# Sums of the first MLP that stay in PSUM, a weight remainder on another engine, and a finer-grained passage into the second MLP

## The chip, the cores and the metric

The kernel runs on one core of one Trainium2 chip. The metric is the time of one execution in microseconds (us) on the device; a version is judged by the median of its runs.

The core's engines each work through an instruction list of their own, in order, and wait for each other through semaphores: TensorE (PE; its weight loads are shown apart as PEld), VectorE (DVE), ScalarE (ACT), GpSimd (POOL) and SyncE (SP, which here only issues transfers). Matmul results go to PSUM, which has eight banks here; everything else lies in SBUF.

## What is computed

Attention with a decay bias, then two MLPs, one after the other, over 1152 tokens:

```python
x = attention(q, k, v, s)              # 2 batches, 8 heads of 64, 576 positions -> [1152, 512]
h = x @ w_in                           # w_in [512, 2048], in float64 at the input
g = np.maximum(0.01 * h, h)
x = g @ w_out                          # w_out [2048, 512]
p = domain_probs / (domain_probs.sum(-1, keepdims=True) + 1e-09)
for e in range(4):                     # second MLP: w1 [4, 512, 1024], w2 [4, 1024, 512]
    h = np.maximum(x @ w1[e], 0.0)
    out += p[:, e:e+1] * (h @ w2[e])
```

## The kernel before, in words

**Numbers.** Every float32 matrix is split in two parts: ACT casts it to the type that the matmul reads (`hi`), and DVE or GpSimd subtracts that from the value (`lo`, the remainder). A product is then three matmuls: hi by hi, lo by hi, hi by lo.

**Tokens.** They are cut in two groups, c = 0 (512 tokens) and c = 1 (640 tokens). The first MLP runs for group 0 by plain matmuls of 512 columns, beginning while attention still runs, and after it for group 1. That second pass and the second MLP's up products for both groups, and its down products for group 0, use a scheme in which a 2 by 2 block product takes seven products instead of eight (`block_products`): four PSUM banks, `ps_u0` to `ps_u3` or `ps_d0` to `ps_d3`, receive four products, then three more are added onto banks 0, 2 and 3. Before the fifth may be added, ACT copies bank 0 to SBUF (`tmp`), and DVE makes sums from that copy. The seven forms of the tokens are tiles `t` (of group 0 or 1), made by `paired_steps` from `x` or `y` by subtractions on DVE, casts on ACT and remainders on DVE; each of the seven has two halves, k = 0 and 1. The seven forms of the weights are tiles `w` with remainders made on GpSimd; the weights of the second MLP's down products get eight forms (`eight`), in two halves of four with additions in the raw weights (`raw`) between them.

**Blocks.** An MLP goes in blocks of four rows of 128 of the hidden dimension: four blocks for the first MLP, f = 0, 4, 8 and 12. A block has two up pieces and two down pieces of weights of 512 KB each. `down1` makes the four down results of a block, in the order d = 0, 2, 1, 3, twelve matmuls each for group 0, and DVE adds each to the sum `y` in SBUF (for block 0 ACT copies it). In the program's order for group 0, between the down products of block 8 and those of block 12 stand the up products of block 12's second pair.

**Order.** Until the end of group 0's pass (`fixed = True`) each engine's order is the program's. From there on a scheduler with a model of the engines decides the order on each engine, unless `keep_in_program_order` is asked for. PSUM banks come from three, and after attention from eight (class `Eight`, which deals them out from two pools in turn). SBUF is given out by pools that are opened and closed as a stack; a pool that is opened where others were closed waits for the last use of what lay there. The raw weights of the second MLP have two buffers (`rawp2`).

**Weights of the first MLP.** `supply` converts them from float64 to float32 and writes them to DRAM (`w_f`), and `late_splits` makes hi and lo of those that are read back late, lo on DVE. The last converted piece is the second down piece of block 12.

**Into the second MLP.** The scheduled part ends with `paired_steps` of group 1 on `y`, whose forms `t` of k = 0 and k = 1 are made in equal steps. Then `second` starts: up products for (pair 0, group 0), (pair 1, group 0), (pair 0, group 1), (pair 1, group 1), then the down products. `next_w` calls `fetch`, which keeps two pieces of weights ahead (`look = 2`).

All these calls are issued through one wrapper class, so that the trace names one line, L43, for nearly all: the rows below are told apart by their tiles.

Of the kernel before, what the change touches and what calls it, by code (L numbers as in the profile page):

```python
# [19 lines left out]
def attention_moe_moe2(ctx: ExitStack, tc: tile.TileContext, q, k, v, s, w_in, w_out, probs, w1, w2, out):  # L20
# [7 lines left out]

    fixed = True

    class InOrder:

# [4 lines left out]
        def __getattr__(self, name):  # L39
            call = getattr(self.engine, name)  # L40

            def issue(*args, **kw):
                ins = call(*args, **kw)  # L43
                return tc.keep_in_program_order(ins) if fixed else ins

            return issue

# [31 lines left out]
    const = ctx.enter_context(tc.tile_pool(name="const", bufs=1))  # L79
    first = ctx.enter_context(ExitStack())  # L80
    rawp = first.enter_context(tc.tile_pool(name="rawp", bufs=RAW))
    ypool = first.enter_context(tc.tile_pool(name="ypool", bufs=1))
    dram = ctx.enter_context(tc.tile_pool(name="dram", bufs=1, space=bass.MemoryType.DRAM))

    def f32(ap):
# [42 lines left out]
    def late_splits():  # L128

        nonlocal reading  # L130
        while len(ready) < CONVERTED:
            n = len(ready)
            if n < min(retired + WB + 2, stored):
                reading, raw = True, kept.pop(n, None)
                if raw is None:
                    raw = load_w(*stream[n][:3])
                    for _ in range(5):
                        yield
                while n >= retired + WB:
                    yield  # L140

                w = wpool.tile([P, 2, 1024], F32R, tag="w", name="w")
                for part in (slice(0, 512), slice(512, 1024)):
                    nc.scalar.copy(w[:, 0, part], raw[:, part])
                    nc.vector.tensor_tensor(w[:, 1, part], raw[:, part], f32(w[:, 0, part]), ALU.subtract)
                ready.append(w.rearrange("p l (a b) -> p l a b", a=stream[n][1][0]))
                reading = False
            else:
                yield
# [113 lines left out]
        return w  # L263

    def eight(raw):

        w = wpool.tile([P, 2, 8, 256], F32R, tag="w", name="w")
        b11, b12, b21, b22 = (raw[:, i * 256 : (i + 1) * 256] for i in range(4))

        def split(i):  # L270
            hi, lo = (w[:, l, i : i + 4].rearrange("p s c -> p (s c)") for l in range(2))
            nc.scalar.copy(hi, raw)
            nc.gpsimd.tensor_tensor(lo, raw, f32(hi), ALU.subtract)

        split(0)
        nc.gpsimd.tensor_tensor(b22, b22, b12, ALU.subtract)
        nc.gpsimd.tensor_tensor(b12, b12, b11, ALU.subtract)
        nc.gpsimd.tensor_tensor(b11, b22, b11, ALU.add)
        nc.gpsimd.tensor_tensor(b21, b21, b11, ALU.subtract)
        split(4)  # L280
        return w

    def first_sevens():

# [85 lines left out]
    def in_steps(ps, pairs):  # L370

        for i, ((wh, wl), (xh, xl)) in enumerate(pairs):
            for j, (a, b) in enumerate(((wh, xh), (wl, xh), (wh, xl))):
                nc.tensor.matmul(ps, a, b, start=(i == j == 0), stop=(i == len(pairs) - 1 and j == 2))
# [6 lines left out]
    x_t, y_t, oacc, touched = [], {}, {}, {}  # L381

    def halves(c):
        return ((0, sizes[0]),) if c == 0 else ((0, half[1]), (half[1], sizes[1]))
# [32 lines left out]
    def down1(f, c, h, w):  # L417

        if f == 0:
            y_t[c] = ypool.tile([P, KD, sizes[c]], F32, tag=f"y{c}", name=f"y{c}")  # L420
        for d in (0, 2, 1, 3):
            for lo, hi in halves(c):
                ps = ps_mm.tile([P, 512], F32, tag="mm", name="ps_d")[:, : hi - lo]
                sl, cols = slice(d * P, (d + 1) * P), slice(lo, hi)
                at_h = [at(x, cols) for x in h] if c == 0 else [at(x, j, cols) for x in h for j in range(2)]
                yield from in_steps(ps, [(at(w[i // 2], i % 2, sl), x) for i, x in enumerate(at_h)])
# [9 lines left out]
    def paired_steps(s, of, pool):  # L436

        n = half[s]
        t = t7[s] = pool.tile([P, 2, 7, 2, n], F32R, tag=f"t7_{s}", name=f"t7_{s}")
        for k in range(2):  # L440
            b11, b12 = of[:, k, :n], of[:, k, n:]
            b21, b22 = of[:, 2 + k, :n], of[:, 2 + k, n:]
            sums = scratch.tile([P, 4 * 320], F32, tag="scratch", name="sums")[:, : 4 * n].rearrange("p (s t) -> p s t", s=4)
            def subtract(*args):
                tc.keep_in_program_order(nc.vector.tensor_tensor(*args, ALU.subtract))

            subtract(sums[:, 1], b12, b11)
            subtract(sums[:, 2], b22, sums[:, 1])
            yield
            subtract(sums[:, 3], b22, b12)  # L450
            subtract(sums[:, 0], b21, sums[:, 2])
            yield
            for i, j, x in ((0, 2, of[:, k::2, :n]), (2, 3, of[:, 2 + k : 3 + k, n:]), (3, 7, sums)):
                hi, lo = (t[:, l, i:j, k] for l in range(2))
                nc.scalar.copy(hi, x)
                subtract(lo, x, f32(hi))
                yield

    def paired_up(w, s, leaky):

        n = half[s]
# [3 lines left out]
        bank = block_products("ps_u", n, lambda a, b: [(at(w, a, k), at(x, b, k)) for k in range(2)])  # L465
        if in_sevens:
# [12 lines left out]
        return ht  # L479
# [26 lines left out]

    def block_products(name, n, operands):

        tmp = scratch.tile([P, 2 * 320], F32, tag="tmp", name="tmp")[:, : 2 * n].rearrange("p (i t) -> p i t", i=2)
# [9 lines left out]
        product(0, 0, 0)  # L519
        nc.scalar.copy(u2, bank[0])  # L520
        product(1, 4, 5)
# [53 lines left out]

    def second(blocks):

        w, h = {}, {}

        def up_part(i, pair, s):  # L580
            if (i, pair) not in w:
                (w[i, pair],) = next_w(1)
            h.setdefault(i, ({}, {}))[pair][s] = paired_up(w[i, pair], s, False)

        for pair, s in ((0, 0), (1, 0), (0, 1), (1, 1)):
# [410 lines left out]
    hpool = None  # L996
    look = 2
    t7pool = scratch = None
    last_mlp = False
    x_t.extend((None, ypool.tile([P, KD, sizes[1]], F32, tag="y1", name="x1")))  # L1000
# [76 lines left out]
    with ExitStack() as phase:  # L1077
# [3 lines left out]
        tokens, rest = paired_steps(0, y_t[0], t7early), None  # L1081
        last = 2 * len(phases[1]) + 32 * (len(phases[1]) - 1) + 16
        for i, _ in enumerate(mlps(phases[1])):
            if i >= 12 and i % 6 == 0:
                next(tokens, None)
            if i >= last:
                rest = rest or paired_steps(1, y_t[1], t7pool)
                if i % 4 == 1 and i < last + 16:
                    next(rest)
        for _ in tokens:  # L1090
            pass
        for _ in rest:
            pass
    first.close()
    last_mlp = True
    rawp = ctx.enter_context(tc.tile_pool(name="rawp2", bufs=2))
# [44 lines left out]
```

## Time and profile before

| | |
|---|---|
| median of 3 runs | 704.36 us (703.07 to 706.07) |
| the profiled execution: time, span of its instructions | 702.2 us, 700.4 us |
| matmul (PE) busy | 678.0 us, 97% of the span, 4496 matmuls |
| weight loads (PEld) busy | 623.2 us, 89% |
| DVE, ACT, GpSimd busy | 476.2, 352.7, 401.3 us |
| chain that ended last | PE 70%, DVE 9%, issue 7%, DMA 6%, ACT 4%, POOL 4% |
| mean granted TensorE clock | 0.997 of full speed |

A busy time is the time in which an engine had an instruction of its own in hand. The idle time in square brackets at the end of a row is the time for which the engine stood before that instruction, with the engine or transfer that ended it. A row with xN holds N instructions that followed each other, and its time runs from the start of the first to the end of the last.

### The profile page before, as it was taken

Reading aid. Unit: us, or ns where it says so; the run is one execution under the profiler, and the core shown is the slowest. Engines: PE = TensorE matmul, PEld = TensorE weight load, DVE = VectorE, ACT = ScalarE, POOL = GpSimd, SP = SyncE. Lnnn points to the kernel's source line nnn. Section 1 sums busy time; section 2 is a strip of 40 time slices with the busy share of each in tenths; the row PEclk is TensorE's granted clock in tenths of the full one; section 3 lists DMA queues with packets and bytes.
Section 4 is the critical chain, followed back from the end, with each engine's and each line's share of the span. In section 5 each row is a group of like instructions: output and inputs, shape, how many; then the busy total and the mean of one; then the engine's idle time right before and its main releaser. Section 6 shows DMA issues by size and latency. Waiting matters only on the chain.

```text
span 700.4 us, 12025 instructions
## 1 busy us (share of the span) xinstructions
PE 678.0 (97%) x4496; PEld 623.2 (89%) x4496; DVE 476.2 (68%) x1043; ACT 352.7 (50%) x726; POOL 401.3 (57%) x382
## 2 busy tenths in 40 slices
PE   8899999899989999998999999999999999999998
PEld 7788777778869999998999989989999899998997
DVE  6878899888798558537764747647656476465573
ACT  5768978966655765534533515415244253252520
POOL 6000213222178888952985949949679499496830
PEclk9999999999999999999999999999999999999999
DMA  8886689746632321101120110201101111112003
GB/s 225 202 221 205 189 233 269 214 138 236 225 125 79 120 91 62 61 1 61 41 53 29 61 61 6 88 30 61 61 1 61 61 34 59 31 61 61 1 31 105
DMA packets 42282, 69.15 MB, mean 99 GB/s; under 512 B 5664, under 2 KB 25904, under 8 KB 42224
## 3 DMA queue, kind: packets, MB, share of 16 engines
q1 hardware_dynamic: 32976, 40.30, 19.7%
q0 software_dynamic: 6016, 20.71, 9.5%
q10 hardware_dynamic: 3232, 7.38, 3.2%
q8 instruction: 35, 0.57, 0.4%
q14 instruction: 23, 0.19, 0.1%
HBM read 57.54 MB, written 10.82 MB: 98 GB/s over the span
## 4 chain that ended last, share of the span: by engine, by line
PE 70%; DVE 9%; issue 7%; DMA 6%; ACT 4%; POOL 4%; ACTq 0%; SPq 0%; POOLq 0%; DVEq 0%
PE ps_d L43 35%; PE ps_u L43 32%; DVE raw L43 2%; DMA r<-in_moe_w_out_dram 2%; DVE w L43 2%; PE ps_sc L43 1%; DVE z L43 1%; POOL w L43 1%; PE ps_o L43 1%; DMA vs<-in_v_dram 1%; ACT z L43 1%; PE ps_pt L43 1%; POOL raw L43 1%; DMA ke<-in_k_dram 1%; ACT w L43 1%
## 5 line engine op out<-in xcount | busy, mean ns | idle before, releaser
L43 PE MATMUL ps_u<-t,w 128*128 128x320 f32 (+1 forms) x1680 | 236.2, 299 | 3.0 <-ACT tmp L43 2.0
L43 POOL TENSOR_TENSOR w<-raw,w 128x512 fp32r<-128x512 f32 (+2 forms) x116 | 181.6, 1584 | 95.6 <-ACT w L43 95.5
L43 PEld LDWEIGHTS ps_u<-t,w 128*128 128x128 f32 x1680 | 229.9, 189 | 4.6 <-ACT tmp L43 2.4
L43 PE MATMUL ps_d<-w,ht 128*128 128x256 f32 (+1 forms) x1164 | 195.2, 326 | 0.0
L43 PEld LDWEIGHTS ps_d<-w,ht 128*128 128x128 f32 x1164 | 173.3, 190 | 18.3
L43 ACT CAST w<-raw 128x512 fp32r<-128x512 f32 (+2 forms) x138 | 98.1, 738 | 137.4 <-PE ps_d L43 88.8
L43 ACT ACTIVATE ht<-ps_u 128x320 fp32r<-128x320 f32 (+2 forms) x160 | 68.5, 436 | 93.1 <-DVE ps_u L43 67.0
L43 PE MATMUL ps_d<-ht,w 128*128 128x320 f32 (+1 forms) x576 | 108.7, 339 | 3.2 <-DVE ht L43 3.2
L43 PEld LDWEIGHTS ps_d<-ht,w 128*128 128x128 f32 x576 | 91.3, 188 | 9.6 <-DVE ht L43 3.6
L43 POOL TENSOR_TENSOR raw<-raw 128x256 f32<-128x256 f32 x120 | 86.2, 738 | 2.2
L43 DVE SCALAR_TENSOR_TENSOR oacc<-ps_d,pn,oacc 128x256 f32<-128x256 f32 (+1 forms) x92 | 51.4, 579 | 46.7 <-PE ps_d L43 46.0
L43 DVE TENSOR_TENSOR ps_u<-ps_u,tmp 128x320 f32<-128x320 f32 (+1 forms) x120 | 56.1, 470 | 34.1 <-PE ps_u L43 32.5
L43 DVE TENSOR_TENSOR tmp<-ps_u,tmp 128x320 f32<-128x320 f32 (+1 forms) x80 | 36.7, 462 | 34.6 <-PE ps_u L43 23.4
L43 DVE SCALAR_TENSOR_TENSOR ht<-ps_u,ht 128x320 fp32r<-128x320 f32 (+1 forms) x112 | 49.7, 455 | 14.3 <-ACT ht L43 14.3
L43 POOL DMA_DIRECT2D w_f<-raw x13 | 8.3, 636 | 86.8 <-DVE raw L43 73.3
L43 PE MATMUL ps_u<-x,w 128*128 128x512 f32 x192 | 56.4, 413 | 0.9 <-DVE x L43 0.9
L43 ACT ACTIVATE z<-z,mn 128x256 f32<-128x256 f32 (+4 forms) x72 | 42.5, 590 | 9.4 <-DVE mn L43 8.5
L43 DVE CUSTOM_DVE_ANT_0 z<-ps_sc,mask 128x256 f32<-128x256 f32 (+4 forms) x72 | 35.9, 499 | 10.4 <-PE ps_sc L43 6.7
L43 POOL TENSOR_TENSOR ht<-sums,ht 128x1024 fp32r<-128x1024 f32 x16 | 38.6, 2410 | 6.5 <-ACT ht L43 6.5
L43 ACT COPY pv<-ps_pt 128x512 f32<-128x512 f32 (+3 forms) x80 | 33.0, 422 | 17.8 <-PE ps_pt L43 17.5
L43 DVE TENSOR_TENSOR ht<-ps_u,ht 128x320 fp32r<-128x320 f32 (+1 forms) x48 | 26.5, 555 | 22.0 <-ACT ps_u L43 21.8
L43 PE MATMUL ps_pt<-ident,z 128*128 128x128 f32 x200 | 34.6, 276 | 6.8 <-ACT pv L43 6.0
(97 smaller groups left out, 774.1 us busy)
## 6 DMA issues: line engine op xcount, KB each, us to landing
raw<-in_moe_w_dram SPq DMA_DIRECT2D x32, 512.0 KB
raw<-w_f SPq DMA_DIRECT2D x21, 512.0 KB
w_f<-raw POOLq DMA_DIRECT2D x13, 512.0 KB, 3.5
r<-in_moe_w_out_dram POOLq DMA_DIRECT2D x6, 1024.0 KB, 7.4
r<-in_moe_w_in_dram POOLq DMA_DIRECT2D x5, 1024.0 KB, 7.6
r<-in_moe_w_in_dram ACTq DMA_DIRECT2D x3, 1024.0 KB
kd<-in_k_dram POOLq DMA_DIRECT2D x8, 288.0 KB, 8.1
kr<-in_k_dram SPq DMA_DIRECT2D x8, 288.0 KB
```

The costliest lines, as they stand in the source:

```text
L43: ins = call(*args, **kw)
```

## The change

It has four parts.

1. **Block 8's down results of group 0 may stay in PSUM** (`stays`, `unread`): where the eight banks are already there when a result is begun, DVE doesn't add it to `y`, and block 12's twelve matmuls for the same d are added onto the same bank.
2. **The last converted piece's remainder** (two instructions of 128 x 512) is made by GpSimd instead of DVE.
3. **Order**: TensorE keeps the program's order through the first two up products of group 1's pass; DVE keeps it at the end of that pass, ACT in parts of the start of the second MLP. The SBUF pool of the two `y` becomes two pools.
4. **Smaller steps into the second MLP**: `paired_steps` of group 1 makes the forms of k = 1 in smaller pieces; `second` begins with the first half of the first down piece's eight forms, and makes their second half and the second down piece only after the second of its four up products, with nothing fetched ahead until then (`look = 0`).

```diff
-                return tc.keep_in_program_order(ins) if fixed else ins
+                return tc.keep_in_program_order(ins) if fixed or self.engine in pinned or (opened2 < 2 and self.engine is tc.nc.tensor) else ins
...
-    ypool = first.enter_context(tc.tile_pool(name="ypool", bufs=1))
+    ypools = [first.enter_context(tc.tile_pool(name=f"ypool{i}", bufs=1)) for i in range(2)]
...
-                    nc.vector.tensor_tensor(w[:, 1, part], raw[:, part], f32(w[:, 0, part]), ALU.subtract)
+                    (nc.gpsimd if n == CONVERTED - 1 else nc.vector).tensor_tensor(w[:, 1, part], raw[:, part], f32(w[:, 0, part]), ALU.subtract)
...
+    def eight_steps(raw):
...
         split(0)
+        yield
         nc.gpsimd.tensor_tensor(b22, b22, b12, ALU.subtract)
...
         split(4)
-        return w
+        yield w
...
-                ps = ps_mm.tile([P, 512], F32, tag="mm", name="ps_d")[:, : hi - lo]
+                onto = unread.pop(d, None) if c == 0 else None
+                ps = onto if onto is not None else ps_mm.tile([P, 512], F32, tag="mm", name="ps_d")[:, : hi - lo]
+                stays = c == 0 and f == DFF // P - 8 and isinstance(ps_mm, Eight)
...
+                if stays:
+                    unread[d] = ps
+                    yield
+                    continue
                 ya = y_t[c][:, d, cols]
...
+        if halved:
...
+            subtract(sums[:, 1], b12, b11)
+            split(0, 1, of[:, 1:2, :n])
+            yield
+            split(1, 2, of[:, 3:4, :n])
+            yield
+            subtract(sums[:, 2], b22, sums[:, 1])
+            subtract(sums[:, 3], b22, b12)
+            subtract(sums[:, 0], b21, sums[:, 2])
+            split(2, 3, of[:, 3:4, n:])
+            split(3, 7, sums)
+            yield
...
+        look, opening_last = 0, True
+        steps = eight_steps(load_w(*stream[len(ready)][:3]))
+        next(steps)
         for pair, s in ((0, 0), (1, 0), (0, 1), (1, 1)):
             up_part(0, pair, s)
+            if (pair, s) == (1, 0):
+                pinned = (tc.nc.scalar,)
+                ready.append(next(steps))
+                fetch(used + 2)
+                look, pinned, opening_last = 2, (), False
```

**Place 1: DVE, while block 12's up products of group 0 run.** `t_1` are the forms of group 1's tokens, `w` the last converted piece, `y` the sum of the down results, `ht` the hidden values. Before:

```order
L43 TENSOR_TENSOR y_1281<-ps_d,y_1281 128x512
L43 TENSOR_TENSOR t_1_2322<-x_100,t_1_2322 128x2x320
L43 TENSOR_TENSOR t_1_2322<-x_100,t_1_2322 128x320
L43 TENSOR_TENSOR y_1281<-ps_d,y_1281 128x512
L43 TENSOR_TENSOR w<-raw,w 128x512 x2
L43 TENSOR_TENSOR t_1_2322<-sums,t_1_2322 128x4x320
L43 TENSOR_TENSOR ht<-ps_u,ht 128x512 x2
```

Now:

```order
L43 TENSOR_TENSOR y_1284<-ps_d,y_1284 128x512
L43 TENSOR_TENSOR sums<-x_103 128x320
L43 TENSOR_TENSOR sums<-x_103,sums 128x320
L43 TENSOR_TENSOR t_1_2325<-x_103,t_1_2325 128x2x320
L43 TENSOR_TENSOR t_1_2325<-x_103,t_1_2325 128x320
L43 TENSOR_TENSOR t_1_2325<-sums,t_1_2325 128x4x320
L43 TENSOR_TENSOR ht<-ps_u,ht 128x512 x2
```

The last two of block 8's four additions to `y` (d = 1 and 3) and the two remainders are gone from ahead of the hidden values' remainders; the first two additions (d = 0 and 2) are still there. The two remainders stand on GpSimd now, behind the first of the remainders of the first seven-form weights.

**Place 2: TensorE, the first up product of group 1's pass**, buffers with their numbers. Before:

```order
L43 MATMUL ps_u0_2541<-t7_1_2322,w7_2378 128x320 x6
L43 MATMUL ps_u1_2542<-t7_1_2322,w7_2378 128x320 x5
L43 MATMUL ps_u2_2543<-t7_1_2322,w7_2378 128x320 x5
L43 MATMUL ps_u3_2544<-t7_1_2322,w7_2378 128x320
L43 MATMUL ps_u1_2542<-t7_1_2322,w7_2378 128x320
```

Now:

```order
L43 MATMUL ps_u0_2540<-t7_1_2325,w7_2379 128x320 x6
L43 MATMUL ps_u1_2541<-t7_1_2325,w7_2379 128x320 x6
L43 MATMUL ps_u2_2542<-t7_1_2325,w7_2379 128x320 x6
L43 MATMUL ps_u3_2543<-t7_1_2325,w7_2379 128x320 x6
L43 MATMUL ps_u0_2540<-t7_1_2325,w7_2379 128x320 x6
```

The sixth matmul of bank 1, the first that reads the remainders of the k = 1 sums, was TensorE's 18th of this product and is its 12th now.

**Place 3: ACT and GpSimd, from the last up products to the first down products of the second MLP.** `w` is a down piece, `w_4015`, `w_4017` and `w_4028` up pieces of the next block, `ps_d_4042`, `ps_d_4044` and `ps_d_4103` bank 0 of down products. ACT before:

```order
L43 CAST ht<-sums 128x1024
L43 COPY tmp<-ps_u_3889 128x320
L43 CAST w<-raw 128x1024 x2
L43 ACTIVATE ht<-ps_u_3889 128x320
...
L43 COPY tmp<-ps_u_3951 128x320
L43 COPY tmp<-ps_d_4042 128x256
L43 CAST ht<-sums 128x1024
L43 CAST w_4015<-raw 128x512
```

ACT now:

```order
L43 COPY tmp<-ps_u_3953 128x320
L43 CAST ht<-sums 128x1024
L43 CAST w<-raw 128x1024 x2
L43 ACTIVATE ht<-ps_u_3953 128x320
...
L43 CAST w_4017<-raw 128x512
L43 CAST w_4017<-raw 128x256
L43 COPY tmp<-ps_d_4044 128x256
L43 COPY tmp<-ps_d_4103 128x256
```

GpSimd before:

```order
L43 TENSOR_TENSOR w<-raw,w 128x1024 x2
L43 TENSOR_TENSOR raw<-raw 128x256 x8
L43 TENSOR_TENSOR ht<-sums,ht 128x1024
L43 TENSOR_TENSOR w<-raw,w 128x1024 x2
L43 TENSOR_TENSOR ht<-sums,ht 128x1024
```

GpSimd now:

```order
L43 TENSOR_TENSOR w<-raw,w 128x1024
L43 TENSOR_TENSOR raw<-raw 128x256 x4
L43 TENSOR_TENSOR ht<-sums,ht 128x1024 x2
L43 TENSOR_TENSOR w<-raw,w 128x1024 x2
L43 TENSOR_TENSOR raw<-raw 128x256 x2
```

On ACT the casts of the next block's up piece, which wait for its transfer, stood behind the first copy of a down bank and stand ahead of it now. On GpSimd the first remainder of the second down piece stood second in the whole stretch and stands behind both `ht` remainders and the second half of the first piece now.

## Rows read from the trace of the kernel before

**Rows 1.** The page, part 1: busy time, share of the span, instructions.

```profile
PE 678.0 (97%) x4496; PEld 623.2 (89%) x4496; DVE 476.2 (68%) x1043; ACT 352.7 (50%) x726; POOL 401.3 (57%) x382
```

**Rows 2.** Waits of PE from 150 us: waiter, releaser: us, times, longest.

```profile
PE ps_d L43 <- DVE ht L43: 3.2, 1, 3.2
PE ps_u L43 <- ACT tmp L43: 2.0, 1, 2.0
PE ps_u L43 <- ACT sums L43: 1.0, 1, 1.0
```

**Rows 3.** Timeline, 196 to 224 us: start, duration, engine, line, instruction, idle before.

```profile
199.36 1.54 POOL L43 TENSOR_TENSOR w<-raw,w 128x512 fp32r<-128x512 f32 x1
199.66 0.68 DVE L43 TENSOR_TENSOR y<-ps_d,y 128x512 f32<-128x512 f32 x1
...
200.26 2.26 DVE L43 TENSOR_TENSOR t<-x,t 128x640 fp32r<-128x640 f32 x2
...
203.05 3.49 DVE L43 TENSOR_TENSOR w<-raw,w 128x512 fp32r<-128x512 f32 x2
203.54 2.45 POOL L43 TENSOR_TENSOR w<-sums,w 128x1024 fp32r<-128x1024 f32 x1 [1.36 <-ACT w L43]
...
203.94 1.98 PE L43 MATMUL ps_d<-ht,w 128*128 128x512 f32 x8
...
204.63 0.59 ACT L43 ACTIVATE ps_u<-ps_u 128x512 f32<-128x512 f32 x1
...
206.47 2.01 DVE L43 TENSOR_TENSOR t<-sums,t 128x1280 fp32r<-128x1280 f32 x1
...
208.40 1.28 DVE L43 TENSOR_TENSOR ht<-ps_u,ht 128x512 fp32r<-128x512 f32 x2
...
209.13 9.36 PE L43 MATMUL ps_d<-ht,w 128*128 128x512 f32 x40 [3.22 <-DVE ht L43]
...
214.03 2.44 DVE L43 TENSOR_TENSOR t<-x,t 128x640 fp32r<-128x640 f32 x1
...
218.33 5.89 PE L43 MATMUL ps_u<-t,w 128*128 128x320 f32 x39
...
218.78 1.89 DVE L43 TENSOR_TENSOR t<-sums,t 128x1280 fp32r<-128x1280 f32 x1
```

**Rows 4.** Timeline, 180 to 196 us.

```profile
189.54 1.28 DVE L43 TENSOR_TENSOR w<-raw,w 128x512 fp32r<-128x512 f32 x2
```

**Rows 5.** Timeline of DVE, 312 to 332 us.

```profile
318.72 1.29 DVE L43 TENSOR_TENSOR y<-ps_d,y 128x320 f32<-128x320 f32 x3 [1.12 <-PE ps_d L43]
...
321.12 0.81 DVE L43 TENSOR_TENSOR t<-y,t 128x640 fp32r<-128x640 f32 x1
...
329.56 1.49 DVE L43 TENSOR_TENSOR t<-sums,t 128x1280 fp32r<-128x1280 f32 x1 [0.19 <-ACT t L43]
```

**Rows 6.** Timeline, 322 to 350 us.

```profile
323.94 5.92 PE L43 MATMUL ps_u<-t,w 128*128 128x256 f32 x48
...
329.52 1.99 ACT L43 CAST w<-raw 128x1024 fp32r<-128x1024 f32 x2
...
331.42 0.64 ACT L43 COPY tmp<-ps_u 128x256 f32<-128x256 f32 x2
...
336.68 0.75 DVE L43 SCALAR_TENSOR_TENSOR sums<-ps_u,sums 128x256 f32<-128x256 f32 x2
...
338.46 1.05 ACT L43 CAST ht<-sums 128x1024 fp32r<-128x1024 f32 x1 [0.27 <-DVE sums L43]
...
341.19 2.40 POOL L43 TENSOR_TENSOR ht<-sums,ht 128x1024 fp32r<-128x1024 f32 x1
...
343.55 4.77 POOL L43 TENSOR_TENSOR w<-raw,w 128x1024 fp32r<-128x1024 f32 x2
...
345.97 2.74 SPq L43 DMA_DIRECT2D raw<-in_moe_w_dram  x2
...
349.50 0.62 ACT L43 CAST w<-raw 128x512 fp32r<-128x512 f32 x1 [1.02 <-DMA raw<-in_moe_w_dram]
```

More of the change, by code (lines that the diff above doesn't have):

```diff
@@ L265, in eight @@
     def eight(raw):
+        steps = eight_steps(raw)
+        next(steps)
+        return next(steps)
+    def eight_steps(raw):
         w = wpool.tile([P, 2, 8, 256], F32R, tag="w", name="w")
@@ L368, in products, with in_steps @@
             nc.tensor.matmul(ps, a, b, start=(i == 0 and not onto), stop=(i == len(pairs) - 1), skip_group_check=onto)
-    def in_steps(ps, pairs):
+    def in_steps(ps, pairs, onto=False):
         for i, ((wh, wl), (xh, xl)) in enumerate(pairs):
             for j, (a, b) in enumerate(((wh, xh), (wl, xh), (wh, xl))):
-                nc.tensor.matmul(ps, a, b, start=(i == j == 0), stop=(i == len(pairs) - 1 and j == 2))
+                nc.tensor.matmul(ps, a, b, start=(i == j == 0 and not onto), stop=(i == len(pairs) - 1 and j == 2), skip_group_check=onto)
             if i < len(pairs) - 1:
@@ L379, in at @@
         return x[(slice(None), 0) + where], x[(slice(None), 1) + where]
-    x_t, y_t, oacc, touched = [], {}, {}, {}
+    x_t, y_t, oacc, touched, unread = [], {}, {}, {}, {}
     def halves(c):
@@ L419, in down1 @@
         if f == 0:
-            y_t[c] = ypool.tile([P, KD, sizes[c]], F32, tag=f"y{c}", name=f"y{c}")
+            y_t[c] = ypools[c].tile([P, KD, sizes[c]], F32, tag=f"y{c}", name=f"y{c}")
         for d in (0, 2, 1, 3):
             for lo, hi in halves(c):
-                ps = ps_mm.tile([P, 512], F32, tag="mm", name="ps_d")[:, : hi - lo]
+                onto = unread.pop(d, None) if c == 0 else None
+                ps = onto if onto is not None else ps_mm.tile([P, 512], F32, tag="mm", name="ps_d")[:, : hi - lo]
+                stays = c == 0 and f == DFF // P - 8 and isinstance(ps_mm, Eight)
                 sl, cols = slice(d * P, (d + 1) * P), slice(lo, hi)
                 at_h = [at(x, cols) for x in h] if c == 0 else [at(x, j, cols) for x in h for j in range(2)]
-                yield from in_steps(ps, [(at(w[i // 2], i % 2, sl), x) for i, x in enumerate(at_h)])
+                yield from in_steps(ps, [(at(w[i // 2], i % 2, sl), x) for i, x in enumerate(at_h)], onto is not None)
+                if stays:
+                    unread[d] = ps
+                    yield
+                    continue
                 ya = y_t[c][:, d, cols]
@@ L434, in attention_moe_moe2, with paired_steps @@
     t7 = {}
-    def paired_steps(s, of, pool):
+    def paired_steps(s, of, pool, halved=False):
         n = half[s]
@@ L457, in paired_steps, with split @@
                 yield
+            if k == 0 and halved:
+                break
+        if halved:
+            b11, b12, b21, b22 = of[:, 1, :n], of[:, 1, n:], of[:, 3, :n], of[:, 3, n:]
+            sums = scratch.tile([P, 4 * 320], F32, tag="scratch", name="sums")[:, : 4 * n].rearrange("p (s t) -> p s t", s=4)
+            def split(i, j, x):
+                hi, lo = (t[:, l, i:j, 1] for l in range(2))
+                nc.scalar.copy(hi, x)
+                subtract(lo, x, f32(hi))
+            subtract(sums[:, 1], b12, b11)
[9 more added lines that the diff above has]
+            yield
     def paired_up(w, s, leaky):
+        nonlocal opened2
         n = half[s]
@@ L465, in paired_up @@
         bank = block_products("ps_u", n, lambda a, b: [(at(w, a, k), at(x, b, k)) for k in range(2)])
+        opened2 += 1
         if in_sevens:
@@ L507, in block_products @@
     def block_products(name, n, operands):
+        nonlocal pinned
         tmp = scratch.tile([P, 2 * 320], F32, tag="tmp", name="tmp")[:, : 2 * n].rearrange("p (i t) -> p i t", i=2)
@@ L519, in block_products @@
         product(0, 0, 0)
+        was, pinned = pinned, (tc.nc.scalar,) if opening_last else pinned
         nc.scalar.copy(u2, bank[0])
+        pinned = was
         product(1, 4, 5)
@@ L576, in second @@
     def second(blocks):
+        nonlocal look, pinned, opening_last
         w, h = {}, {}
@@ L583, in up_part @@
             h.setdefault(i, ({}, {}))[pair][s] = paired_up(w[i, pair], s, False)
+        look, opening_last = 0, True
+        steps = eight_steps(load_w(*stream[len(ready)][:3]))
+        next(steps)
         for pair, s in ((0, 0), (1, 0), (0, 1), (1, 1)):
             up_part(0, pair, s)
+            if (pair, s) == (1, 0):
[3 more added lines that the diff above has]
+                look, pinned, opening_last = 2, (), False
         for i, (e, _, _) in enumerate(blocks):
@@ L998, in attention_moe_moe2 @@
     t7pool = scratch = None
-    last_mlp = False
-    x_t.extend((None, ypool.tile([P, KD, sizes[1]], F32, tag="y1", name="x1")))
+    last_mlp = opening_last = False
+    x_t.extend((None, ypools[1].tile([P, KD, sizes[1]], F32, tag="y1", name="x1")))
     with ExitStack() as phase:
@@ L1083, in attention_moe_moe2 @@
         for i, _ in enumerate(mlps(phases[1])):
+            pinned = (tc.nc.vector,) if i + 1 >= last else ()
             if i >= 12 and i % 6 == 0:
@@ L1086, in attention_moe_moe2 @@
             if i >= last:
-                rest = rest or paired_steps(1, y_t[1], t7pool)
-                if i % 4 == 1 and i < last + 16:
+                rest = rest or paired_steps(1, y_t[1], t7pool, True)
+                if i - last in (1, 3, 5, 7, 9, 10, 13):
                     next(rest)
@@ L1093, in attention_moe_moe2 @@
             pass
+        pinned = ()
     first.close()
```

2 lines of the change are left out of this document (1 added, 1 removed).

## The prediction

> **What bounds the kernel now.** I read the page's busy times first, then PE's waits, then the timeline around each of them, then the order of the instructions before and after.
>
> PE is busy for 97% of the span and no other engine for more than 68% [rows 1], so only time in which PE stands still can be won. From 150 us on, where the change begins to act, PE waits three times for more than a moment: 3.2 us for DVE's remainders of the hidden values `ht`, 2.0 us for ACT's copy `tmp` and 1.0 us for ACT's `sums` [rows 2]. That is 6.2 us, 0.9% of the whole, and the most that the change can win. The number of matmuls is the same in both programs.
>
> The sum is made against the profiled execution, 702.2 us, which lies 2.16 us below the median of 704.36 us; I carry the sum over to the median unchanged. A measurement of this kernel can tell about 0.5% (3.5 us) from no change: 700.84 and 707.88 are the bounds for "faster" and "slower".
>
> **First wait, at 209.13 us (parts 1 and 2).** The diff speaks of results that stay in PSUM; the order shows that only two do (d = 1 and 3), since DVE's additions for d = 0 and 2 are still there. DVE's list ahead of `ht` loses two additions (0.60 from the start of one, 199.66, to the next instruction, 200.26; the other lies in the 0.53 between 202.52, the end of the two `t`, and 203.05) and the two remainders `w`, 203.05 to 206.47, 3.42 [rows 3]. Together 4.6 us: the first `ht` remainder moves from 208.40 to 203.8. The second is then bound by ACT, which ends at 204.63 + 0.59 = 205.22, so it is ready at about 205.9. PE goes on from 203.94 at 0.23 per matmul (9.20 over 40, from 209.13 to 218.33) and wants the first after eight matmuls, at 205.8, and the second some three later, at 206.5. Both are in time, by 1.9 and 0.6. GpSimd has to bring `w` by 205.6 and 206.2 instead: it can start at 200.90, when its instruction of 1.54 ends, and two of that length end at 204.0, 1.6 early [rows 3]. Removed: **-3.2**, the whole wait. Were GpSimd 2 us later than this, part of it would return; the third rival prices that.
>
> **What is late next: the first product of group 1's pass.** Behind `ht` DVE works through the same list as before, 3.74 earlier (the second `ht` ended at 209.68 and now at 205.94). Its last `t<-sums` ended at 218.78 + 1.89 = 220.67 and will end at 216.93. PE had just avoided waiting for it: its 18th matmul of this product came at 218.33 + 17 x 0.15 = 220.8 (5.89 over 39, [rows 3]). Now PE keeps the program's order, and the matmul that reads these remainders is the 12th. It is wanted at 203.94 + 48 x 0.23 + 11 x 0.15 = 216.6. **+0.4** (217.0 with the semaphore). Bounds: 0, if the `t` of 2.44 at 214.03 runs as its like did at 321.12, in 0.81 [rows 3, 5]; +1.6, if GpSimd's shifted work slows the list by another half of the 2.44. I take the middle value, since all neighbours keep their lengths.
>
> **Second wait, at 331.84 us (parts 3 and 4).** Call 323.94, the first up product of the second MLP, X. PE ran 5.92 there and stood still for 2.0, until X + 7.9, because ACT's copy `tmp`, 0.36 long, came behind two casts `w` of together 1.99 (329.52) [rows 2, 6]. One of these casts is gone from ahead of it, which looks like a gain. But the order shows that the copy also waits for DVE, whose last `t<-sums` ended at 329.56 + 1.49 = 331.05, X + 7.1 [rows 5]. That end decides. DVE's list from 318.72 on is the same work, 12.3 us long with about 1 us of idle, cut into one more piece [rows 5]. The new order fills some idle (the `t<-sums` of k = 0 runs ahead of the last two additions to `y`), but puts more behind the last addition: its own 0.49, three sums of together 1.4, ACT's cast of 1.26, now covered by only one short `t`, and the 1.49 of the last remainder, 4.7 in all. The last addition starts at about X + 2.9, so the remainders end at X + 7.6, the copy at X + 8.0 and PE goes on at X + 8.1. **+0.2**: the wait stays. Bounds: -0.4, with the end at X + 7.1 less half a microsecond of idle filled; +0.6, if each of the smaller pieces costs another 0.1 to 0.2. A gain of the whole 2.0 is excluded by DVE's list alone.
>
> The two banks of four now come one pair after the other and no longer in turn, so that DVE's additions after the copy are less covered by PE's matmuls: I add **+0.3** for two such moments, from one DVE instruction of 0.37 (336.68, two in 0.75) less what the six matmuls between hide. Bounds 0 and +0.8.
>
> **Third wait, for `sums`.** It came from GpSimd's and ACT's long list at that place, from which the second half of the first down piece is gone: **-1.0** [rows 2].
>
> **The second down piece comes late.** GpSimd now has, in this order, both `ht` remainders (2.40 each), the second half of the first piece, then the first of the second (2.39 each, 4.77 at 343.55) [rows 6]. The second `ht` needs the last product of (pair 1, group 0). PE reaches its end after 84 matmuls of 256 columns (0.12 each, 5.92 over 48), 36 of 320 (0.147) and 2.8 of waits: X + 18.2. Then nine DVE instructions at 0.37 make 3.4, with 0.2 of semaphores X + 21.8; the cast 1.05 (338.46); GpSimd 2.40 + 2.39 + 2.39: X + 30.0 to 30.2. PE wants that remainder after 84 matmuls of 256 columns, 84 of 320, some 31 of the down products and the 2.8: 10.1 + 12.3 + 3.7 + 2.8 = X + 28.9. **+1.3**. Bounds 0 and +2.5 (one `ht` more or less on GpSimd).
>
> **The next block's up piece comes late, and ACT stands.** Its transfer needs the buffer that GpSimd reads until X + 27.7. From issue to landing it took 3.53 (345.97 to 349.50), and ACT already waited 1.02 for it [rows 6]. It lands at X + 31.2. Before, the copy `tmp<-ps_d` of the first down product stood ahead of the casts that wait for this; now it stands behind two of them. Casts 0.9, copy 0.36: X + 32.5. PE, held until X + 30.2, wants the copy two matmuls later, at X + 30.4. **+2.1**. Bounds 0 and +3.
>
> **The sum:** -3.2 + 0.4 + 0.2 + 0.3 - 1.0 + 1.3 + 2.1 = +0.1. Forecast **704.5 us**, no change that can be told; its own range is 702.8 to 706.3.
>
> **Rivals.** *Faster: the weights are in time.* If the last two terms are nothing, because GpSimd gets the weights' halves done between the `ht` or the buffer comes free earlier, -3.3 is left: 701.1 us, and 699.8 with the lower bounds of the small terms. For it: the same supply held before. Against it: GpSimd's list is strict, and its lengths are measured. Chance 0.30.
>
> *Slower: the lateness goes on.* At the opening of the next block the copy `tmp<-ps_u` stands behind two casts of its second down piece (1.99 for such two, [rows 6]). If its raw weights land later than 1.99 + 0.36 = 2.35 before PE wants the copy, PE waits again, for at most one transfer, 3.53. My count puts that landing within half a microsecond of the point. Price up to +3: 707.5 us. Against it: before, PE didn't wait there. Chance 0.12.
>
> *Slower: DVE and GpSimd hold each other up.* The two remainders `w` took DVE 1.28 at 189.54 and 3.49 at 203.05, with an instruction of 2.45 on GpSimd beside them from 203.54 [rows 3, 4]. The two that go to GpSimd now lie beside DVE's list ahead of `ht`. If DVE stands still while each of them runs (1.54 each), the first `ht` comes at up to 206.9, PE wants it at 205.8 and the second soon after, so that 1.8 of the 3.2 return and 0.5 more at the 12th matmul: 706.8 us. Against it: DVE's two `t` at 200.26 already ran partly beside such an instruction. The Trainium skill ("SBUF — State Buffer", "Who interferes with whom") says that DVE reading two SBUF operands and GpSimd share one pair of ports and that whoever has it shuts the other out for the whole instruction; the row at 203.05 agrees with it, in that 3.49 is about 1.28 and most of a 2.45. Chance 0.08.
>
> Forecast 0.45, rivals 0.30, 0.12 and 0.08, 0.05 for what I don't see. About half of the first rival lies below 700.84, a third of the second above 707.88: faster 0.18, same 0.71, slower 0.11. The range from 700.6 to 707.4 leaves out the far ends of both.
>
> **What would show it.** Right: PE no longer waits at 209; a wait of about 0.4 for DVE's `t` some 8 us later; about 2 us for `tmp` at the start of the second MLP, with DVE's last `t<-sums` ending X + 7.6; no wait for `sums`; then waits for GpSimd's `w` (about 1.3) and for ACT's `tmp` behind a cast that waited for a transfer (about 2.1). Wrong: if GpSimd's order lets the second piece be ready before X + 28.9, the time falls to 701; if PE waits near 205 for DVE or GpSimd, or again in the second block, it rises. A copy `tmp` that ends before X + 6 would show that DVE's list was counted wrongly.

## The result, and the profile after

The changed kernel takes 707.11 us (median of 19 runs, 702.59 to 712.71), the kernel before in the same job 704.36 us (19 runs): a ratio of 1.0065 with a 95% interval of 1.004 to 1.0091. It is slower, by a little more than such a measurement can tell; 704.5 was forecast, with no change that can be told. The means given below leave out runs that lie more than 1.5% above the fastest of their kernel.

The profiled execution took 705.3 us, its span 703.5. The first view is again PE's waits from 150 us (engine and tile that waits, releaser: us, times, longest), which answers to [rows 2]:

```profile
PE ps_u L43 <- DVE t L43: 2.4, 1, 2.4
PE ps_u L43 <- ACT tmp L43: 2.1, 1, 2.1
PE ps_d L43 <- ACT tmp L43: 1.8, 1, 1.8
...
PE ps_d L43 <- POOL w L43: 1.0, 1, 1.0
PE ps_d L43 <- DVE ht L43: 0.4, 1, 0.4
```

Three waits of 6.2 us have become five of 7.8 (a wait of attention, 1.0 us before and 1.2 now, is left out of both). The wait for `ht` has nearly gone (3.2 to 0.4), that for `sums` is gone, that for the first `tmp` has stayed. New are one for DVE's `t` and two at the first down products. PE's own timeline in the changed kernel shows where they stand:

```profile
203.42 9.38 PE L43 MATMUL ps_d<-ht,w 128*128 128x512 f32 x40 [0.40 <-DVE ht L43]
212.63 1.77 PE L43 MATMUL ps_u<-t,w 128*128 128x320 f32 x11
216.81 9.87 PE L43 MATMUL ps_u<-t,w 128*128 128x320 f32 x55 [2.40 <-DVE t L43]
...
322.43 5.92 PE L43 MATMUL ps_u<-t,w 128*128 128x256 f32 x48
330.46 16.14 PE L43 MATMUL ps_u<-t,w 128*128 128x256 f32 x102 [2.12 <-ACT tmp L43]
...
354.05 0.51 PE L43 MATMUL ps_d<-w,ht 128*128 128x256 f32 x2 [1.05 <-POOL w L43]
356.37 20.54 PE L43 MATMUL ps_d<-w,ht 128*128 128x256 f32 x114 [1.82 <-ACT tmp L43]
```

The 2.40 comes before the 12th matmul of group 1's first product, where the forecast had 0.4. Why DVE is late there is seen in DVE's and GpSimd's rows of the same execution, which answer to [rows 3]:

```profile
192.95 0.68 DVE L43 TENSOR_TENSOR y<-ps_d,y 128x512 f32<-128x512 f32 x1
...
196.53 6.82 POOL L43 TENSOR_TENSOR w<-raw,w 128x512 fp32r<-128x512 f32 x4
196.85 3.42 DVE L43 TENSOR_TENSOR t<-x,t 128x640 fp32r<-128x640 f32 x2
...
200.19 2.57 DVE L43 TENSOR_TENSOR t<-sums,t 128x1280 fp32r<-128x1280 f32 x1
...
202.68 1.28 DVE L43 TENSOR_TENSOR ht<-ps_u,ht 128x512 fp32r<-128x512 f32 x2
...
203.32 2.39 POOL L43 TENSOR_TENSOR w<-sums,w 128x1024 fp32r<-128x1024 f32 x1
...
203.88 2.18 DVE L43 TENSOR_TENSOR sums<-x 128x320 f32<-128x320 f32 x1
...
212.29 2.41 POOL L43 TENSOR_TENSOR w<-sums,w 128x1024 fp32r<-128x1024 f32 x1
...
212.65 2.10 DVE L43 TENSOR_TENSOR pn<-pn,prow 128x36 f32<-128x36 f32 x1
...
215.28 1.48 DVE L43 TENSOR_TENSOR t<-sums,t 128x1280 fp32r<-128x1280 f32 x1
```

With GpSimd at work beside them for 6.82 us, the two `t` took 3.42 (2.26 before) and the `t<-sums` 2.57 (2.01 before). The `sums<-x` beside GpSimd's next instruction took 2.18, and the last step of the probabilities `p`, `pn<-pn,prow`, which has only 36 columns, took 2.10 and ended with GpSimd's `w<-sums` at 214.7. In the kernel before, the same two took 0.50 and 0.20:

```profile
209.60 0.50 DVE L43 TENSOR_TENSOR sums<-x 128x320 f32<-128x320 f32 x1
...
218.06 0.20 DVE L43 TENSOR_TENSOR pn<-pn,prow 128x36 f32<-128x36 f32 x1
```

The `ht` remainders, one of whose operands is in PSUM, kept their 1.28. From the first of the two remaining additions to `y` (192.95) to the end of the last `t<-sums` (216.76) DVE took 23.8 us. Before, the same stretch with two more additions and the two `w` was 24.9 (195.76 to 220.67). So 4.6 us of instructions were taken out of DVE's list and it grew shorter by 1.1. This comparison is of one execution with one.

One more thing has changed from before: the granted clock of TensorE. Windows of the changed kernel (us, then busy time and count of PE, PEld, DVE, ACT, POOL; the clock is the third number from the end):

```profile
218.00:222.00 4.00, 4.00 (x19) 4.00 (x18) 1.55 (x4) 1.85 (x6) 4.00 (x3) 0.57 0.13 33
222.00:226.00 4.00, 4.00 (x29) 4.00 (x29) 2.65 (x6) 3.65 (x10) 3.19 (x4) 1.00 0.66 229
...
330.46:334.20 3.74, 3.74 (x19) 3.74 (x19) 2.45 (x6) 1.04 (x3) 3.51 (x4) 0.56 0.00 0
```

From 1.2 us after the end of the wait of 2.40, PE ran 19 matmuls in four microseconds, and in the next four 29 of the same kind; the granted clock was 0.57 in the first four, most of that stretch at the lower of its two levels (1.2 of 2.4 GHz). After the 2.12 it was 0.56. In the profiled execution of before the clock did not fall after 3.22 and 1.98 us of standing still.

### The profile page after: what moved, and what is told of

It reads as the page before. It is cut to its first block, busy times and chain, and to the rows that moved or that the text cites. A ratio compares the mean times of both kernels' runs of the same rounds, so it can differ in the third digit from the quotient of the medians.

```text
span 703.5 us, 12028 instructions
## 1 busy us (share of the span) xinstructions
PE 680.7 (97%) x4496; PEld 625.6 (89%) x4496; DVE 476.8 (68%) x1040; ACT 353.7 (50%) x727; POOL 404.8 (58%) x384
## 4 chain that ended last, share of the span: by engine, by line
PE 68%; DVE 10%; DMA 7%; issue 6%; POOL 5%; ACT 4%; SPq 0%; ACTq 0%; POOLq 0%; DVEq 0%
PE ps_d L43 32%; PE ps_u L43 31%; POOL w L43 2%; DVE raw L43 2%; PE ps_sc L43 2%; DMA raw<-in_moe_w_dram 2%; PE ps_o L43 1%; PE ps_pt L43 1%; DVE t L43 1%; DVE w L43 1%; POOL raw L43 1%; DMA r<-in_moe_w_out_dram 1%; DMA vs<-in_v_dram 1%; DVE sums L43 1%; DVE z L43 1%
## 5 line engine op out<-in xcount | busy, mean ns | idle before, releaser
L43 PE MATMUL ps_u<-t,w 128*128 128x320 f32 (+1 forms) x1680 | 239.6, 301 | 4.7 <-DVE t L43 2.4
L43 POOL TENSOR_TENSOR w<-raw,w 128x512 fp32r<-128x512 f32 (+2 forms) x118 | 186.4, 1599 | 94.4 <-ACT w L43 94.4
L43 PEld LDWEIGHTS ps_u<-t,w 128*128 128x128 f32 x1680 | 233.1, 192 | 6.3 <-ACT tmp L43 2.8
L43 POOL TENSOR_TENSOR ht<-sums,ht 128x1024 fp32r<-128x1024 f32 x16 | 38.6, 2415 | 14.4 <-ACT ht L43 14.4
L43 ACT COPY pv<-ps_pt 128x512 f32<-128x512 f32 (+3 forms) x80 | 33.1, 423 | 16.3 <-PE ps_pt L43 16.1
```

## Experiments

Each version in the table was run 12 times; a ratio is to the kernel before on the same chip, with its 95% interval. The mean clock is that of its executions. PE's waits are the sum of those after 200 us in the profiled execution.

| version | median us | ratio (interval) | mean clock | PE's waits, us |
|---|---|---|---|---|
| before once more | 704.21 | 1.0019 (0.9981 to 1.0057) | 0.9948 | 6.8 |
| changed once more | 706.83 | 1.0051 (1.002 to 1.0082) | 0.9946 | 8.6 |
| changed, remainder on DVE | 708.48 | 1.009 (1.0057 to 1.0124) | 0.9912 | 8.3 |
| changed, TensorE's order free | 706.50 | 1.0073 (1.0041 to 1.0105) | 0.9942 | 6.9 |
| changed, ACT's order free | 702.24 | 1.002 (0.9982 to 1.0058) | 0.9950 | 4.7 |
| changed without part 4 | 702.49 | 0.9992 (0.9959 to 1.0026) | 0.9958 | 3.7 |
| before, `tmp` apart | 699.07 | 0.9944 (0.9911 to 0.9978) | 0.9967 | 2.7 |
| the same again | 698.01 | 0.9958 (0.9922 to 0.9993) | 0.9972 | 0.5 |
| mixed | 696.87 | 0.9917 (0.989 to 0.9945) | 0.9978 | 0.3 |
| mixed again | 696.56 | 0.9921 (0.9895 to 0.9948) | 0.9982 | 0.6 |
| mixed, remainder on DVE | 698.03 | 0.9931 (0.9898 to 0.9964) | 0.9972 | 0.0 |

**The kernel before, once more.** No edit.

> The kernel before, unchanged, taken once more so that the granted TensorE clock of each of its executions is known (for the changed kernel the 19 executions show a mean clock of 0.988 to 1.0 and times that fall with it by some 0.72 us for each 0.001, 703.2 us at 1.0). Theory C, the changed kernel's new waits are what makes the clock fall: before's mean clock is 0.997 or more in nearly every execution, and its times lie at about 701 to 703 us at that clock. Rival, the clock falls as often in the kernel before and the extra time is the waits of PE alone: mean clock about 0.9945 here too, and a similar spread of times.

Measured: mean clock 0.9948, times 697.73 to 710.58. Its profiled execution has a fall of the clock too, after a wait of 3.80 for `ht`. Theory C, by which the kernel before runs at 0.997 or more, does not stand: its mean clock was 0.9948 here and 0.9951 to 0.996 beside the other versions, against 0.9945 and 0.9946 for the changed kernel, which at 0.72 us for 0.001 is 0.2 to 1.1 us. Within one kernel the clock explains much of the spread (19 executions: 712.71 us at 0.988, 702.89 at 1.0).

**The remainder on DVE again.**

```diff
-                    (nc.gpsimd if n == CONVERTED - 1 else nc.vector).tensor_tensor(...)
+                    nc.vector.tensor_tensor(...)
```

> The changed kernel with the last converted piece's two remainders on DVE again. Theory P, DVE's instructions that read two SBUF operands are held up while GpSimd works (t x2 took 3.42 us after and 2.26 before, t<-sums 2.57 and 2.01): with GpSimd's two instructions gone from beside them these are short again, so the two remainders cost DVE only about 3.4 - 1.7, and PE's first wait (0.4 after) is 1.5 to 2.3. Rival, those lengths have another cause: they stay, and the first wait is 0.4 + 3.4 = 3.8 or more. Time: 0 to 2 us above or below the changed kernel.

Measured: 2.67 for `ht` and 0.62 for `t`, neither figure in place, but nearer to theory P than to 3.8. DVE's timeline in this version:

```profile
197.51 0.68 DVE L43 TENSOR_TENSOR y<-ps_d,y 128x512 f32<-128x512 f32 x1
...
204.19 1.28 DVE L43 TENSOR_TENSOR w<-raw,w 128x512 fp32r<-128x512 f32 x2
205.40 3.67 DVE L43 TENSOR_TENSOR t<-sums,t 128x1280 fp32r<-128x1280 f32 x1
...
219.47 1.79 DVE L43 TENSOR_TENSOR t<-sums,t 128x1280 fp32r<-128x1280 f32 x1
```

The two `w` took 1.28 here, not the 3.49 of [rows 3], and the `t<-sums` behind them 3.67, not 2.01. The stall has moved by one instruction. From 197.51 to 221.26 the list took 23.75 us, against 23.81 with the remainders on GpSimd: by this pair of executions, part 2 shortened DVE's list by nothing.

**The two engines by themselves.** The kernel's body is replaced by the instructions that the expectation names.

> None of the reference's work: the output is zeros. On one pair of engines alone: eight subtractions of 128x320 on DVE from two SBUF operands with nothing beside them; six of 128x1024 on GpSimd alone; then eight of the first kind beside six of the second; then sixteen on DVE with one operand in PSUM beside six on GpSimd. Theory P, the two engines hold each other up where DVE reads two SBUF operands: 0.48 us each alone, 2.4 each on GpSimd alone; beside each other DVE's take up to 2.4 longer and the pair needs about the sum of both, 8 x 0.48 + 6 x 2.4; with the PSUM operand they keep their 0.49 and GpSimd its 2.4. Rival, the long rows have another cause: all keep their lengths beside each other.

Measured, DVE and GpSimd alone, then beside each other, then with the operand in PSUM (`ps`):

```profile
4.18 4.16 DVE L39 TENSOR_TENSOR sums<-x,sums 128x320 f32<-128x320 f32 x8
...
27.69 16.29 DVE L39 TENSOR_TENSOR sums<-x,sums 128x320 f32<-128x320 f32 x8 [0.97 <-POOL big L52]
...
46.48 8.37 DVE L43 TENSOR_TENSOR sums<-ps,sums 128x320 f32<-128x320 f32 x16 [0.97 <-POOL big L52]
```

```profile
10.83 14.43 POOL L47 TENSOR_TENSOR big<-x,big 128x1024 f32<-128x1024 f32 x6
...
27.73 15.37 POOL L47 TENSOR_TENSOR big<-x,big 128x1024 f32<-128x1024 f32 x6
...
46.52 14.45 POOL L47 TENSOR_TENSOR big<-x,big 128x1024 f32<-128x1024 f32 x6
```

Eight subtractions took DVE 4.16 us alone and 16.29 beside GpSimd, which lost 0.9 of 14.4. With one operand in PSUM GpSimd lost nothing (14.45), and DVE took 0.52 each, as long as with both in SBUF and nothing beside it. The pair needed 16.3, less than the 18.6 of the sum; theory P holds as to the mechanism, and it is DVE that pays.

**TensorE's order free.**

```diff
-                return tc.keep_in_program_order(ins) if fixed or self.engine in pinned or (opened2 < 2 and self.engine is tc.nc.tensor) else ins
+                return tc.keep_in_program_order(ins) if fixed or self.engine in pinned else ins
```

> The changed kernel without the order that TensorE keeps in the first two up products of group 1's pass: the matmul that reads the late remainders is the 18th again. My theory of the wait of 2.4 us for DVE's t: what is late is DVE's list, and six matmuls of 0.15 cover 0.9 of it, so the wait is 1.5 us and the time 1 us less; if the clock falls after that wait because it is long, it also falls more seldom, another 0.5 to 1.5 us less. Rival: the wait stays at 2.4 since the order on PE decides nothing; time as the changed kernel's.

Measured: the wait for `t` is 1.50, as expected, in front of the 18th matmul. The time's interval covers the changed kernel's, so the gain of 0.9 us itself is not shown.

**ACT's order free.**

```diff
             if (pair, s) == (1, 0):
-                pinned = (tc.nc.scalar,)
                 ready.append(next(steps))
```

> The changed kernel with ACT's order free after the second up product of the second MLP: the copy tmp<-ps_d stands ahead of the casts that wait for the transfer again. My theory: PE's wait of 1.8 us for tmp behind these casts goes, that of 1.05 us for GpSimd's w stays, time 1.5 to 2 us below the changed kernel. Rival: the late transfer itself is what PE waits for, and the same 1.8 us comes back within the next 30 us under another name; time as the changed kernel's.

Measured: 702.24 us, and both waits at the first down products are gone, not one. PE's waits after 200 us in this version:

```profile
PE ps_u L43 <- DVE t L43: 2.4, 1, 2.4
PE ps_u L43 <- ACT tmp L43: 2.3, 1, 2.3
```

The copy stands ahead of the late casts again; and ACT casts the second down piece ahead of the last `ht`, so that GpSimd has its remainder at 347.4 and no longer at 354.0. Nothing came back under another name. The changed kernel was not run beside this version; the versions with the remainder on DVE and with TensorE's order free, which have both waits and ran with it on one chip, have means 6.2 and 3.8 us longer (708.65 and 706.23 against 702.48).

**The changed kernel once more**, on the chip of the next three.

> The changed kernel once more, on the chip of the three runs beside it, as what they are compared with. Expected from its 19 executions: 703.2 us at a granted clock of 1.0 and some 0.72 us more for each 0.001 of clock below it; PE's waits after 200 us 0.4, 2.4, 2.1, 1.05 and 1.8 us, 7.8 together.

Measured: the waits for `t` and the two for `tmp` at 2.37, 2.12 and 1.90, that for `w` at 1.03, that for `ht` 0.94, and one of 0.23 for `sums`; 3.6 us slower than before by the ratio.

**Without part 4.** `second` and `paired_steps` of group 1 as before, no order kept on ACT and DVE:

```diff
-        look, opening_last = 0, True
-        steps = eight_steps(load_w(*stream[len(ready)][:3]))
-        next(steps)
...
-            if (pair, s) == (1, 0):
-                pinned = (tc.nc.scalar,)
-                ready.append(next(steps))
-                fetch(used + 2)
-                look, pinned, opening_last = 2, (), False
```

> The changed kernel without part 4 and the orders of part 3 for ACT and DVE: the second MLP is opened as before, the first MLP's part of the change is kept. Theory, part 4 brings the two waits at the first down products: they are gone (1.05 and 1.8), the wait of 1.0 us for sums is back, those of 0.4, 2.4 and 2.0 stay; waits 5.8 us together instead of 7.8, time 2 us below the changed kernel and about that of the kernel before (6.2). Rival, those waits come from the earlier end of the first MLP (weights that are asked for no earlier): they stay without part 4 too.

Measured: 702.49 us, the two waits at the down products gone; 1.98 for `tmp` and 1.71 for `t` are left, that for `ht` is gone where 0.4 was expected to stay, and that for `sums` did not come back. Against the changed kernel beside it this is 4.2 us less in the mean (701.90 and 706.05). What is left out here made the kernel slower, and of it ACT's kept order is enough: the version with that order free has all the rest of part 4, and both waits are gone there too. From the second MLP's first up product to the end, the profiled executions took 376.78 us with ACT's order free and 377.00 here, 381.07 in both of the changed kernel, and 376.46 and 376.43 in those of the kernel before.

**The copies `tmp` in a pool of their own**, opened where `t7early` is, in the kernel before:

```diff
+    tmps = ctx.enter_context(tc.tile_pool(name="tmps", bufs=2, side="right"))
...
-        tmp = scratch.tile([P, 2 * 320], F32, tag="tmp", name="tmp")[...]
+        tmp = tmps.tile([P, 2 * 320], F32, tag="tmp", name="tmp")[...]
```

> The kernel before, with the copies tmp in a pool of their own, opened ahead of group 1's pass, so that the copy at the start of the second MLP doesn't wait until DVE has read the last sums of the pool that was closed. Theory, that memory is what the copy waits for, and the casts ahead of it hardly count: PE's wait of 2.0 us goes, and some of it comes back as waits of under 0.6 us for DVE's sums in tmp, since DVE still works on the forms of group 1: time 1 to 2 us below the kernel before. Rival, the wait moves to DVE's additions and stays 2.0 in all.

Measured: 0.9944, and 4.7 us less in the means (698.32 against 703.06), where 1 to 2 was expected; the wait for `sums` is gone as well. The timeline at the start of the second MLP, which answers to [rows 6]:

```profile
320.04 12.13 PE L43 MATMUL ps_u<-t,w 128*128 128x256 f32 x96
...
321.33 0.37 ACT L43 COPY tmp<-ps_u 128x256 f32<-128x256 f32 x1
...
326.15 2.00 ACT L43 CAST w<-raw 128x1024 fp32r<-128x1024 f32 x2
...
326.58 1.48 DVE L43 TENSOR_TENSOR t<-sums,t 128x1280 fp32r<-128x1280 f32 x1
...
332.68 3.49 PE L43 MATMUL ps_u<-t,w 128*128 128x320 f32 x22 [0.52 <-ACT tmp L43]
```

The copy begins 1.3 us after PE's start, 5 us before DVE's last `t<-sums` begins, and PE runs 96 matmuls on end. So the copy needs nothing that DVE makes there: what tied it to DVE was memory.

**Parts 1 and 2 with `tmp` apart ("mixed")**, part 4 left out, the order of TensorE, DVE and ACT free.

> Parts 1 and 2 of the change alone, TensorE's order left to the scheduler, and the copies tmp in the pool of their own. By the waits measured one at a time: 0.45 for ht, 1.5 for DVE's t, none for tmp, 1.0 or less for sums; 3 us together instead of 6.2: 2.5 to 3.3 us below the kernel before. Rival, the terms don't add since DVE's list is one chain and each wait removed makes the next one longer: within 1.5 us of the kernel before.

Measured: 696.87 us, 0.9917, and 5.9 us below the kernel before in the means (697.13 against 703.06), about twice what was expected, with one wait in the profile after 200 us:

```profile
PE ps_u L43 <- DVE t L43: 0.3, 1, 0.3
```

This version beats both kernels. The last three ran on one chip.

> The mixed version once more (parts 1 and 2, TensorE's order free, copies tmp in a pool of their own), beside the two below on one chip. Expected as measured: PE's waits after 200 us together under 1 us, ratio to the kernel before 0.992.

> The mixed version with the last converted piece's two remainders on DVE. What is tested is whether part 2 shortens DVE's list at all. Theory P: from the first of the two additions to y ahead of it to the end of the last t<-sums DVE takes 23.8 us in every run with the remainders on GpSimd and 23.75 in the one with them on DVE, since what GpSimd holds up moves to other instructions; so here 23.8 too, the wait for ht some 1.7 us longer and that for t shorter by as much, and a time within 0.3% of the mixed version. Rival, the two remainders cost DVE their 3.4 us: the list takes 26 to 27 us and the time is 2 to 3.4 us above the mixed version.

> The kernel before with the copies tmp in a pool of their own, once more, beside the mixed version. If parts 1 and 2 are worth the 2.8 us of the first wait that I forecast, it is 2 to 3 us above the mixed version; if they only move DVE's list about, within 1.5 us of it, as its waits of 2.2 and 0.5 against 0.3 and the times at a clock of 1.0 (696.0 and 695.75) suggest.

Measured: 0.9921, 0.9931 and 0.9958, means of 696.6, 696.8 and 698.4 us. With the remainders on DVE the time is the same within the spread, so the rival (26 to 27 us of list) is out; but the list took 23.0, and the wait for `ht` was none where 1.7 more was expected. The kernel before with `tmp` apart is 1.8 us above the mixed version, between the two marks that were set (1.5, and 2 to 3), and such a difference of means is known to about 2 us: whether parts 1 and 2 win anything once `tmp` lies apart is not shown, and no version has part 1 alone.

The kernel before with `tmp` apart had a wait of 2.17 for `ht` in one execution and none in the other. DVE's rows of the one and of the other:

```profile
199.54 1.28 DVE L43 TENSOR_TENSOR w<-raw,w 128x512 fp32r<-128x512 f32 x2
200.74 3.69 DVE L43 TENSOR_TENSOR t<-sums,t 128x1280 fp32r<-128x1280 f32 x1
```

```profile
202.36 1.28 DVE L43 TENSOR_TENSOR w<-raw,w 128x512 fp32r<-128x512 f32 x2
203.56 1.48 DVE L43 TENSOR_TENSOR t<-sums,t 128x1280 fp32r<-128x1280 f32 x1
```

In the first, GpSimd's remainder `w<-sums` of 2.53 us began at 200.55, just ahead of the `t<-sums`; in the second, where it had waited longer for ACT's cast, at 204.95, behind it and beside the `ht` remainders, which have an operand in PSUM. So the wait that the change was measured against is not a fixed 3.2: in four executions of that list, the last two with `tmp` apart, it was 3.22, 3.80, 2.17 and 0, and the list itself took 24.9, 24.4, 24.4 and 23.0 us. The 23.8 of the changed kernel lies inside that.

## Why the prediction was wrong

**First wait: -3.2 forecast, -2.8 measured.** The `ht` remainders came 1.8 us later against PE than forecast. The slack of the first was 1.3 and not 1.9, since PE could go on only 0.73 after its start (208.40 to 209.13 in [rows 3]); so most of the 1.8 was covered, and a wait of 0.40 was left (0.94 in the second profile).

**"What is late next": +0.4 forecast, +2.4 measured. This is the step that failed.** It said that DVE works through the same list 3.74 earlier, "since all neighbours keep their lengths". They did not. Of the 3.42 that the two `w` took on DVE, only 1.28 were their own; the rest was the time for which GpSimd held them up, and that passed on to the `t`, the `sums` and `pn`. The last was on no list of the forecast: it stood two instructions ahead of the last `t<-sums` and took 1.9 us more than before, though its result is first read at 357.4 us. Whether the last remainders would have come sooner with `pn` elsewhere, or GpSimd would only have held up the next instruction, no run tests. One `t`, 2.44 before, ran in 0.81, as the term's lower bound had it. Moving the two to GpSimd gave GpSimd more to hold DVE up with. The two places together gave 0.4 and not 2.8. The row that says so was in hand, 1.28 in [rows 4] against 3.49 in [rows 3]; I used it for the third rival at a chance of 0.08 and went on to subtract the whole 3.42 in the sum. That rival's time, 706.8, is close to the measured one and its mechanism is the one found, but it had the loss at the wait for `ht` and not at the 12th matmul.

The Trainium skill ("SBUF — State Buffer", "Who interferes with whom") says that a DVE instruction with two inputs in SBUF contends with a GpSimd instruction that reads SBUF, that one with at most one such input does not, and that the order of issue decides who is blocked. The runs by themselves agree: 0.52 us each with the operand in PSUM, 2.04 (16.29 over 8) with both in SBUF, and, as to the order, 3.69 for a `t<-sums` that began behind GpSimd's instruction and 1.48 for one that began ahead of it. In the probe, where instructions follow closely on both engines, it was DVE that lost, 12.1 us against GpSimd's 0.9.

**Second wait: +0.2 forecast, +0.14 measured** (2.12), and for the reason given: DVE's last `t<-sums` ended at 328.44 + 1.49 = 329.93, X + 7.5 (7.6 forecast). What was not seen is that the end of DVE's list only matters through memory, which two lines take away.

**Small waits: +0.3 forecast, none and 0.23 measured. Third wait: -1.0, right.**

**Second down piece: +1.3 forecast, +1.05 measured. Next block's up piece: +2.1 forecast, +1.82 measured.** Mechanism, place and size were right. GpSimd had the remainder at 354.0, X + 31.6 instead of 30.2, and PE wanted it at X + 30.6 instead of 28.9; both are later than forecast, mainly because PE's 19 matmuls behind the 2.12 took 3.74 at the lower clock, 1.4 more than at 0.123 each, so the difference kept its size. That ACT's kept order stood behind both waits was not said; the run with that order free shows it. The casts ahead of the copy waited 4.51 for their transfer:

```profile
349.26 4.73 POOL L43 TENSOR_TENSOR w<-raw,w 128x1024 fp32r<-128x1024 f32 x2
...
355.12 0.92 ACT L43 CAST w<-raw 128x512 fp32r<-128x512 f32 x2 [4.51 <-DMA raw<-in_moe_w_dram]
...
355.95 0.64 ACT L43 COPY tmp<-ps_d 128x256 f32<-128x256 f32 x2
```

**The sum.** +0.1 was forecast; the terms as measured make -2.82 + 2.40 + 0.14 - 1.02 + 1.05 + 1.82 = +1.6. The versions give the same split: what was done at the second MLP was worth +2.9 in the forecast and +4.2 in the means (706.05 against 701.90), the parts ahead of it -2.8 in the forecast and -1.2 in the means (701.90 against the 703.06 of before in that job). The profiled executions agree on the second MLP: from X to the end they took 4.6 us more (381.07 against 376.46 and 376.43), 2.0 of it by the terms at that place and 1.4 by the lower clock behind the 2.12; 1.2 stays open. Over all executions the mean clock adds 0.2 to 1.1. With the waits that makes 1.8 to 2.7 of a measured 2.75 (medians of the first comparison) to 4.6 us (its ratio). The rest stays open; the first wait's own spread, 0 to 3.8, is as large. The rival that lateness goes on into the next block did not occur: PE's waits list none after 357 us.

## What to carry to other kernels

Before a step is moved from one engine to another because it is long there, see whether it is long by itself: compare it with the same instruction where the other engine is idle. If it is long because of the other engine, moving it there moves the stall to its neighbours. And where a copy at the start of a stage waits for an engine that it takes nothing from, look at what lay in its memory: a pool opened earlier was worth 0.4 to 0.6% here, where the whole change lost 0.5 to 0.65%.

## What the runs showed of the hardware beyond that

How long DVE and GpSimd hold each other up changes from one execution to the next: whether GpSimd's remainder starts 0.2 us ahead of it or 1.4 us behind decides between 3.69 and 1.48 us for one DVE instruction. And the clock's fall is no cost of one wait that these runs would let one foresee. It followed the 2.40 in the changed kernel, but not the 2.43 in the version with ACT's order free. The 55 matmuls behind that wait took 9.87 us (above) in the one and 8.53 in the other:

```profile
217.13 8.53 PE L43 MATMUL ps_u<-t,w 128*128 128x320 f32 x55 [2.43 <-DVE t L43]
```

Over 12 executions the versions with few waits of PE have the higher mean clock (0.9967 to 0.9982 with up to 2.7 us of waits, 0.9912 to 0.9946 with 7.8 and more), so a wait that is taken away may pay somewhat more than its length; no run separates the two.
